# MLP2's second product shared out by products instead of by token tiles

## The chip, the cores and the metric

One NeuronCore of one Trainium2 chip runs the whole program in one launch. The metric is the device time of that launch in microseconds: the median of the timed runs is 855.25 us before the change (three runs, 855.01 to 855.51). The profile is of one further execution of the same kernel, which took 852.9 us and whose instructions span 851.2 us.

## The reference

Windowed attention (4 batches, 8 heads, 576 positions, head size 64; four heads with a window of 32, four with a dilated one) gives x, 2304 tokens by 512. Two MLPs follow, one on the other's result, each with an inner width of 2048:

```
x = attention(q, k, v)                                   # 2304 x 512
h = x @ moe_w_in;   g = where(h > 0, h, exp(min(h, 0)) - 1);   x = g @ moe_w_out
h = x @ moe2_w_in;  g = h * clip(h + 3, 0, 6) / 6;             out = g @ moe2_w_out
```

Inputs and result are float32, and the products hold float32 precision: each operand is split into a high part (rounded to the matmul's format) and a low part (the rest), and three matmuls (high-high, high-low, low-high) stand for one.

## The kernel before

**Stages.** Attention and MLP1 run together over five blocks of tokens (up to about 470 us of the profile). Then MLP2 runs over NC = 3 blocks c of 768 tokens. Both of its products use Strassen's scheme in Winograd's form: a product of 2x2 blocks is made from seven products k = 0 to 6 of sums of blocks instead of eight. The inner width 2048 is walked in KP = 8 steps j of 256.

**The first product** (`gemm2nd`, L932) makes, for a block c and a step j, seven products of 128x384 (six matmuls each, L956) in a chain through three PSUM banks q, p, r; ScalarE copies q aside (L983), VectorE adds (L991), ScalarE and VectorE apply the activation (L1001, L1007). The result is the tile g of step j. Its weights stream from DRAM through a ring `w` of six buffers of 512 KB (`ws_i`, L911); the right operands x lie in SBUF, loaded per block (L879).

**The second product** (`tile2`, L1040) goes by token tiles: i = 0, 1, 2, each of two rows of 128 tokens. For one tile and one step, VectorE forms five sums of g's blocks (L1055, L1059, L1061), ScalarE casts the high parts (`ga`, `gz`, L270), VectorE or GpSimd forms the low parts (L273), and TensorE runs 7 products x 3 passes = 21 matmuls of 256 columns (L1094). The seven results of a tile, 1 KB per partition each, accumulate over the eight steps in four PSUM banks. Four of the seven right operands (`w`, L922) stay in SBUF for all blocks; the other three stream through the ring `w` too (`ws_x`), 12 loads of 512 KB for a pass over all steps, and there are two passes per block: one for tiles 0 and 1 together, one for tile 2.

**Order.** In each block the first product comes first. Tiles 0 and 1 then run alone and fill all eight banks. Tile 2 runs beside the next block's first product (4 banks and the q, p, r of that product); after the last block it runs alone. During the first product of block 1 the right operands of block 2 are also made (`rights`, L784): loads `xq`, sums, casts, stores `rhs`. At the end of a tile `y2_out` (L1156) combines the seven sums into four quarters of output (two ScalarE copies, L1188, eight VectorE adds, L1193) and stores each as 128 KB.

**Who decides the order.** `Plan.run` (L122) simulates the five engines and the DMA queue with fixed costs when the program is built. Each job has a key (its due time, here from `times2`, L828); an engine takes the ready job of the smallest key unless another can start clearly earlier. What it chooses is the order in which each engine's instructions are written; on the chip every engine then works through its list in order and waits for its semaphores. All DMAs are issued by SyncE (SP) on one queue. A DMA's end is assumed as issue + 1.4 us + its own share of the queue + 1.6 us (L190, L191). Rings of buffers (`y` with five, shared by MLP1, the temporaries t and the outputs; `ghl`, `gz`, `ga` with three each) hold a writer back until a buffer is free.

**The 16 loads of resident weights** (`load_w1`, L915) take the place of MLP1's second weights, and are free to go as each of those is used for the last time.

Of the kernel before, what the change touches and what calls it, by code (L numbers as in the profile page):

```python
# [20 lines left out]
P = 128  # L21
# [17 lines left out]
CFG = dict(  # L39
    LAGT=0.23, LAGE=0.07, LAND=1.6,  # L40
# [9 lines left out]
    BUFS=dict(y=5, ghl=3, q=1, k=1, v=1, pt=1, g=8, w=6, gz=3, ga=3),  # L50
    WARM=46.0,
    FROM=1.6,
    END=2, ENDW=8,
# [3 lines left out]
    LAG2=1,  # L57
# [142 lines left out]
def tile_window_attention_two_mlps(  # L200
# [50 lines left out]
    w2d = (  # L251
        dram.tile([P, KP * 7, 2, EH], F32, name="w2di"), dram.tile([P, KP * 4, 2, EH], F32, name="w2do"),
        dram.tile([P, KP * 3, 2, EH], F32, name="w2dx"),
    )
# [11 lines left out]
    RINGS["all"] = Ring(list(BANKS.values()))  # L266
    ENG = {"D": nc.vector, "A": nc.scalar, "P": nc.gpsimd}
# [93 lines left out]
    def stage(key, x, dst, users, need, n=EH, pool=stg, ring="stg"):  # L361

        r = {}

        def hi(e):
            r["w"] = take(pool, ring, [P, 2, n], F32R, f"stg{next(turns)}")
# [5 lines left out]
        su = []  # L372
# [35 lines left out]
    def weights2(j, key, step):  # L408
# [4 lines left out]
        def pair(z, k0, dst, steps):  # L413
# [14 lines left out]
            1, key + step * 0.25, lambda k: w2d[1][:, 4 * j + k] if k < 4 else w2d[2][:, 3 * j + k - 4], (  # L428
# [246 lines left out]
    def tile1(b, i):  # L675
# [34 lines left out]
        def hi(e):  # L710
            r["g"] = take(gp, "ghl", [P, 2, T1], F32R, f"ghl{b}_{i}")
            copy(e, r["g"][:, 0, :], r["e"])
# [15 lines left out]
        hu, eu, gu = Users(), [], []  # L728
# [58 lines left out]
    def rights_of(c, p, k0, start, pool, ring, spool, sring):  # L787

        r, us = {}, [[], []]
        after = [*start] + [x2_done[n, k] for n in range(NB1) for k in (p, p + 2) if A1[n] < (c + 1) * 2 * N1 and A1[n + 1] > c * 2 * N1]  # L790

        def load(e):
            for n in range(2):
                r[n] = take(pool(), ring, [P, 2, N1], F32, f"xq{c}_{p}_{n}")
# [4 lines left out]
        ld = job(k0 - 6.0, load, {"S": 0.84}, after, 2.0, [(RINGS[ring], u) for u in us])  # L799
        for u in us:  # L800
            u.append(ld)
        t = {f"b{n + 1}{h + 1}": lambda n=n, h=h: r[n][:, h] for n in range(2) for h in range(2)}

        def put(k, x, key, users, need):
# [8 lines left out]
            k0, 0.3, t, {v: us[int(v[1]) - 1] for v in t}, dict.fromkeys(t, [ld]), (  # L813
# [11 lines left out]
    GEMM, TILE = 42 * C["R"](N1), 21 * C["R"](EH)  # L825
    MM = 6 * C["R"](N1)

    def times2():  # L828

        t = TB[NB1]  # L830
        for c in range(NC):
            rest = [(c - 1, 2, j) for j in range(KP)] if c else []
            if rest:
                second2[rest[0]] = t, t + 12 * C["R"](EH)
                t += TILE
            for j in range(KP):
                first2[c, j] = t
                if j + 1 < len(rest):
                    second2[rest[j + 1]] = t - 0.1, t + 4.5 * MM
                period2[c, j] = GEMM + (TILE if j + 1 < len(rest) else 0.0)  # L840
                t += period2[c, j]
            t -= 2 * MM
            L = CFG["LAG2"]
            for j in range(KP + L):
                for i, n in ((0, j), (1, j - L)):
                    if 0 <= n < KP:
                        second2[c, i, n] = t, t + 12 * C["R"](EH)
                        t += TILE
# [40 lines left out]
    def load_stream():  # L889
# [6 lines left out]
        for c, i, j in second2:  # L896
            for k in range(3):
                m = "x", c, 0 if i < 2 else 2, (3 * j + k) // 2
                uses[m] = min(uses.get(m, 1e9), second2[c, i, j][0])
        prev = start3  # L900
        for m, key in sorted(uses.items(), key=lambda x: x[1]):
            n = m[-1]
            src, done = (
                (w2d[0], [w2_done[0, x // 7, x % 7] for x in (2 * n, 2 * n + 1)]) if m[0] == "i" else
                (w2d[2], [w2_done[1, x // 3, 4 + x % 3] for x in (2 * n, 2 * n + 1)])
            )
# [8 lines left out]
    def load_w1(i):  # L915
        j, k = divmod(i, 2)
        key = min(second2[0, 0, j][0], second2[0, 1, j][0]) - 30.0
# [7 lines left out]
        w2j[i, 1] = job(key + 0.1, load, {"S": 0.42}, [last[1], *(w2_done[1, j, 2 * k + c] for c in range(2))], 1.3, [(RINGS["w1"], u)])  # L925
# [114 lines left out]
    def tile2(c, i, j):  # L1040

        b = NG * c + i
        k1, k2 = second2[c, i, j]
        lead = k1 - CFG["LEAD2"]
        r = {}

        parts = lambda: g_t[c, j].rearrange("p k t i n -> p (k t) i n")[:, :, i]

        def sums(n):
            def fn(e):  # L1050
                if n == 0:
                    r["f"] = take(gp, "ghl", [P, 5, P], F32, f"gf{b}_{j}")
                z, f = parts(), r["f"]
                if n == 0:
                    ENG[e].tensor_tensor(  # L1055
                        out=f[:, 0:2], in0=z[:, 0:2], in1=z[:, 3:4].to_broadcast([P, 2, P]), op=ALU.add
                    )
                elif n == 1:
                    ENG[e].tensor_tensor(out=f[:, 2], in0=z[:, 0], in1=z[:, 2], op=ALU.add)  # L1059
                else:  # L1060
                    ENG[e].tensor_tensor(out=f[:, 3:5], in0=z[:, 1:3], in1=z[:, 0:4:3], op=ALU.subtract)  # L1061
            return fn

        def a_hi(e):
            r["a"] = take(p2["z"], "ga", [P, 2, 2, P], F32R, f"ga{b}_{j}")
            copy(e, r["a"][:, 0], parts()[:, 0:4:3])

        def a_lo(e):
            sub(e, r["a"][:, 1], parts()[:, 0:4:3], r["a"][:, 0].bitcast(F32))

        def z_hi(e):
            r["z"] = take(p2["z"], "gz", [P, 2, 5, P], F32R, f"gz{b}_{j}")
            copy(e, r["z"][:, 0], r["f"])

        def z_lo(e):
            sub(e, r["z"][:, 1], r["f"], r["z"][:, 0].bitcast(F32))

        def g2(banks):
            def fn(e):
                ms = ys.setdefault(("m", b), {})  # L1080
                for n in banks:
                    if j == 0:
                        y = ps.tile([P, 2, EH], F32, tag=m_users[b][n].tag, name=f"m{b}_{n}")
                        for z, (k, _, _) in enumerate(PRODS[n]):
                            ms[k] = y[:, z]
                    for z, (k, ka, kb) in enumerate(PRODS[n]):
                        if kb < 4:
                            w = w_t[1, 2 * j + kb // 2, 1][:, kb % 2]
                        else:
                            m = 3 * j + kb - 4  # L1090
                            w = stream["x", c, 0 if i < 2 else 2, m // 2][:, m % 2]
                        for s, (a, v) in enumerate(PASSES):
                            g = r["a"][:, a, ka] if ka < 2 else r["z"][:, a, ka - 2]
                            nc.tensor.matmul(  # L1094
                                ms[k], g, w[:, v, :], start=(j == 0 and z == 0 and s == 0),
                                stop=(j == KP - 1 and z == len(PRODS[n]) - 1 and s == 2),
                            )
            return fn

        fu, au, zu = [], [], []  # L1100
        gd = g_done[c, j] + ([x for k in rights_done if k[0] == 2 for x in rights_done[k]] if (c, i, j) == (1, 0, 0) else [])
        o = lambda n: {"D": C["D"](n), "P": C["P"](n)}
        before = LAST.get("sums")
        gate = gates.get((c, i, j))
        s = [job(lead, sums(0), {"D": C["D"](N2)}, [*gd, before and (before, -9.0), gate and (gate, -9.0)], 0, [(RINGS["ghl"], fu)])]
        LAST["sums"] = s[0]
        s += [job(lead + 0.01 * n, sums(n), o(P) if n == 1 else {"D": C["D"](N2)}, [s[0]]) for n in (1, 2)]
        j5 = job(lead + 0.1, a_hi, {"A": C["A"](N2)}, gd, 0, [(RINGS["ga"], au)])
        j6 = job(lead + 0.15, z_hi, {"A": C["A"](5 * P)}, s, 0, [(RINGS["gz"], zu)])
        j7 = job(lead + 0.2, a_lo, o(N2), [j5])  # L1110
        j8 = job(lead + 0.3, z_lo, {"D": C["D"](5 * P)}, [j6])
        g_users[c, j] += [*s, j5, j7]
        fu += [*s, j6, j8]
        prev = LAST.get(b) if j or i == 2 else prod[c, KP - 1, 3]
        if j == 0:
            m_users[b] = [Users() for _ in PRODS]
        xs = [("x", c, 0 if i < 2 else 2, n) for n in sorted({(3 * j + k) // 2 for k in range(3)})]
        need = [j7, j8, w2j[2 * j, 1], w2j[2 * j + 1, 1], *(stream_j[m] for m in xs)]
# [270 lines left out]
```

## Time and profile before

| | |
|---|---|
| median of the runs | 855.25 us (855.01 to 855.51) |
| profiled execution, its span | 852.9 us, 851.2 us |
| TensorE busy | 828.0 us (97%), 5749 matmuls |
| VectorE, ScalarE, GpSimd busy | 606.9 us (71%), 453.1 us (53%), 51.2 us (6%) |
| DMA | 227.85 MB, mean 268 GB/s |
| granted TensorE clock, mean | 0.995 |
| streamed loads in MLP2 | 84 `ws_i` and 72 `ws_x`, 512 KB each |

Busy shares are means over stages with different limits. In MLP2 the stages are, in us of the span: first product of block 0 from about 470 to 537, tiles 0 and 1 alone to 578, block 1's first product with tile 2 to 668, alone to 710, block 2's first product with tile 2 to 788, and all that is left of the second product to 847.

### The profile page before, as it was taken

The numbers are of one execution on the slowest core, as the hardware profiler recorded it, in microseconds if no ns is written. First come the engines' busy times: TensorE is split into PE (matmuls) and PEld (weight loads), VectorE is DVE, ScalarE is ACT, GpSimd is POOL, SyncE is SP. The second block draws the span as 40 slices with busy tenths as digits, with TensorE's granted clock in tenths as the row PEclk, the third lists the DMA queues.
The fourth block names the chain that finished last, engine by engine and source line by source line (L and its number), as shares of the span: only waits on it lengthen the run. The fifth ranks groups of instructions, "written<-read, shape, count | busy, mean of one in ns | idle before, by whom it ended". The sixth has DMA issues, their size and how long they took to land.

```text
span 851.2 us, 15721 instructions
## 1 busy us (share of the span) xinstructions
PE 828.0 (97%) x5749; PEld 749.2 (88%) x5749; DVE 606.9 (71%) x1337; ACT 453.1 (53%) x1048; POOL 51.2 (6%) x85
## 2 busy tenths in 40 slices
PE   7999999999999999999999799999999999999997
PEld 6888888888888888888899799999899999999997
DVE  5998878777777777666456285677767878656796
ACT  3999766666566767452344254444445444444442
POOL 2000010000100000000000000000101000000010
PEclk9999999999999999999999999999999999999999
DMA  9994457787777787644699987969989958888456
GB/s 355 407 368 168 144 197 271 241 261 234 237 268 264 257 270 236 228 120 144 230 356 377 352 273 243 401 197 321 384 285 373 397 193 293 271 260 285 143 170 232
DMA packets 85452, 227.85 MB, mean 268 GB/s; under 512 B 9088, under 2 KB 21376, under 8 KB 85376
## 3 DMA queue, kind: packets, MB, share of 16 engines
q1 hardware_dynamic: 85376, 226.86, 76.6%
q8 instruction: 45, 0.74, 0.3%
q14 instruction: 31, 0.25, 0.1%
HBM read 171.51 MB, written 55.31 MB: 266 GB/s over the span
## 4 chain that ended last, share of the span: by engine, by line
PE 89%; DMA 7%; DVE 1%; ACT 1%; issue 0%; SPq 0%; DVEq 0%; ACTq 0%
PE h L667 23%; PE yp L723 23%; PE m L1094 19%; PE cq L956 11%; PE cr L956 6%; DMA ws_i<-w2di 3%; PE cp L956 3%; PE po L583 2%; PE ps L509 2%; DMA raw<-in_w_in_dram 1%; DMA x2d<-y 1%; DMA ws_x<-w2dx 1%; DMA k<-in_k_dram 1%; PE pp L559 1%; DVE o L1193 0%
## 5 line engine op out<-in xcount | busy, mean ns | idle before, releaser
L723 PE MATMUL yp<-ghl,w 128*128 128x512 f32 (+1 forms) x960 | 213.3, 371 | 0.0
L667 PE MATMUL h<-xh,w 128*128 128x512 f32 (+1 forms) x640 | 195.4, 371 | 1.8 <-DVE e L701 1.6
L723 PEld LDWEIGHTS yp<-ghl,w 128*128 128x128 f32 x960 | 166.3, 189 | 30.0
L667 PEld LDWEIGHTS h<-xh,w 128*128 128x128 f32 x640 | 117.2, 189 | 22.2 <-DVE e L701 1.8
L956 PE MATMUL cq<-x,ws_i 128*128 128x384 f32 x576 | 115.8, 344 | 7.1 <-ACT t L983 5.0
L667 PE MATMUL h<-xl,w 128*128 128x512 f32 (+1 forms) x320 | 117.8, 368 | 0.0
L956 PEld LDWEIGHTS cq<-x,ws_i 128*128 128x128 f32 x576 | 102.0, 190 | 10.1 <-ACT t L983 6.8
L687 ACT ACTIVATE e<-h 128x512 f32<-128x512 f32 (+1 forms) x80 | 44.4, 555 | 121.3 <-PE h L667 117.6
L701 DVE SCALAR_TENSOR_TENSOR e<-e,h 128x512 f32<-128x512 f32 (+1 forms) x80 | 50.5, 632 | 69.4 <-ACT e L690 69.1
L1094 PE MATMUL m<-w,gz 128*128 128x256 f32 x648 | 95.1, 283 | 0.0
L270 ACT CAST gz<-gf 128x640 fp32r<-128x640 f32 x72 | 52.1, 727 | 80.3 <-PE m L1094 62.4
L1094 PEld LDWEIGHTS m<-w,gz 128*128 128x128 f32 x648 | 86.0, 192 | 0.0
L273 DVE TENSOR_TENSOR gz<-gf,gz 128x640 fp32r<-128x640 f32 x72 | 59.6, 830 | 29.6 <-ACT gz L270 29.2
L667 PEld LDWEIGHTS h<-xl,w 128*128 128x128 f32 x320 | 60.4, 189 | 9.8 <-DVE xl L590 0.3
L983 ACT COPY t<-cq 128x384 f32<-128x384 f32 x72 | 34.4, 478 | 60.9 <-PE cq L956 52.6
L1001 ACT ACTIVATE g<-t 128x384 f32<-128x384 f32 x72 | 37.8, 525 | 51.2 <-DVE t L991 51.2
L1094 PE MATMUL m<-ws_x,gz 128*128 128x256 f32 x432 | 63.5, 283 | 0.0
L956 PE MATMUL cr<-x,ws_i 128*128 128x384 f32 x288 | 57.9, 345 | 0.6 <-DMA ws_i<-w2di 0.6
L1007 DVE SCALAR_TENSOR_TENSOR g<-g,t 128x384 f32<-128x384 f32 x72 | 40.4, 560 | 24.3 <-ACT g L1001 23.3
L1094 PEld LDWEIGHTS m<-ws_x,gz 128*128 128x128 f32 x432 | 57.0, 192 | 0.0
L273 DVE TENSOR_TENSOR ghl<-e,ghl 128x512 fp32r<-128x512 f32 (+1 forms) x80 | 50.9, 637 | 3.7 <-ACT ghl L270 1.3
L956 PEld LDWEIGHTS cr<-x,ws_i 128*128 128x128 f32 x288 | 52.6, 194 | 0.9 <-DMA ws_i<-w2di 0.9
(89 smaller groups left out, 1170.0 us busy)
## 6 DMA issues: line engine op xcount, KB each, us to landing
ws_i<-w2di SPq DMA_DIRECT2D x84, 512.0 KB, 4.9
ws_x<-w2dx SPq DMA_DIRECT2D x72, 512.0 KB, 5.2
raw<-in_w_in_dram SPq DMA_DIRECT2D x32, 512.0 KB, 6.1
raw<-in_w_out_dram SPq DMA_DIRECT2D x32, 512.0 KB, 5.9
x<-rhs SPq DMA_DIRECT2D x42, 384.0 KB, 8.2
w2di<-stg SPq DMA_DIRECT2D x56, 256.0 KB, 4.5
rhs<-stg SPq DMA_DIRECT2D x28, 384.0 KB, 6.1
q<-in_q_dram SPq DMA_DIRECT2D x18, 512.0 KB, 5.7
```

Source lines behind the costliest of these rows:

```text
L270: (nc.scalar.copy if e == "A" else nc.vector.tensor_copy)(out=out, in_=in_)
L273: ENG[e].tensor_tensor(out=out, in0=in0, in1=in1, op=ALU.subtract)
L509: nc.tensor.matmul(pe[c * KW:(c + 1) * KW, n, :], t["q"][:, c, n, :], kk[:, c], start=not pe_masks, stop=not pe_masks or n == NB - 1)
L667: nc.tensor.matmul(h, w[:, a, c * P:(c + 1) * P], x[b][:, c, :], start=(c == 0 and s == 0), stop=(c == KD - 1 and s == 2),)
L687: nc.scalar.activation(out=r["e"], in_=r["h"], func=AF.Relu, scale=-1.0)
L701: nc.vector.scalar_tensor_tensor(out=r["e"], in0=r["e"], scalar=-1.0, in1=r["h"], op0=ALU.add, op1=ALU.max)
L723: nc.tensor.matmul(ys[b, n], w[:, a, n * P:(n + 1) * P], g[:, c, :], start=(i == 0 and s == 0), stop=(i == KF - 1 and s == 2),)
L956: nc.tensor.matmul(r[b], w[:, a, p * P:(p + 1) * P], x2[c, k, p][:, z, :], start=start and p == 0 and n == 0, stop=p == 1 and n == 2, skip ...
L983: nc.scalar.copy(out=r[n], in_=r[b])
L1001: nc.scalar.activation(out=g_t[c, j][:, k, t].rearrange("q i n -> q (i n)"), in_=r[src], func=AF.Relu, bias=3.0)
L1007: nc.vector.scalar_tensor_tensor(out=z, in0=z, scalar=6.0, in1=r[src], op0=ALU.min, op1=ALU.mult)
L1094: nc.tensor.matmul(ms[k], g, w[:, v, :], start=(j == 0 and z == 0 and s == 0), stop=(j == KP - 1 and z == len(PRODS[n]) - 1 and s == 2),)
```

## The change

The second product is shared out by products. In each block, the five products 3, 2, 4, 0, 1 run alone for all three tiles together (pass `b`), and products 5 and 6 run for all three tiles beside the next block's first product (pass `e`), after the last block alone. One job is now one product of one step for three tiles: PART = 9 matmuls of 256 columns. The number of matmuls is the same.

- PSUM: products 3, 2, 4, 0, 1 of tiles 0 and 1 take a bank each; tile 2's halves pair up in banks "32", "40", "1x" (eight banks). Pass `e` takes three: "5", "6" and "56" for tile 2. A half of tile 2 is read once the later product of its bank is done.
- Operands: sums are 384 wide, one per product (`plus`, three in pass `b`); `less` overwrites two blocks of g in place before pass `e`. The high and low parts of each product go through one ring `gc` of seven buffers (the three of `ghl` and four new ones).
- Streamed weights: pass `b` needs one of the three (4 loads of 512 KB per block), pass `e` two (8 loads): 12 per block in place of 24.
- Outputs: a ring `o` of nine buffers of 128 KB in place of `y`. All three tiles' outputs are combined at the end of pass `b` (6 copies, 18 adds of one quarter each); the quarters (1,1) and (0,0) then wait in their buffers for products 5 and 6.
- Loads: a resident weight with i >= 6 is put behind the first product of step (i - 6) // 2 of block 0, less 9 us of the plan. The two loads of `xq` become two jobs, and block 2's right operands are staged through `gc`.

```diff
-    BUFS=dict(y=5, ghl=3, q=1, k=1, v=1, pt=1, g=8, w=6, gz=3, ga=3),
+    BUFS=dict(y=5, ghl=3, q=1, k=1, v=1, pt=1, g=8, w=6, gc=4, o=9),
+    PASS = dict(b=((3, 1, 4), (2, 0, 3), (4, 4, 1), (0, 2, 2), (1, 3, 0)), e=((5, 5, 6), (6, 6, 5)))
+    HALF = {3: ("32", 0), 2: ("32", 1), 4: ("40", 0), 0: ("40", 1), 1: ("1x", 0), 5: ("56", 0), 6: ("56", 1)}
...
+            if c:
+                second2[c - 1, "e", 0] = t, t + PART
+                t += 2 * PART
             for j in range(KP):
                 first2[c, j] = t
+                period2[c, j] = GEMM
+                if c and j + 1 < KP:
+                    second2[c - 1, "e", j + 1] = t - 0.1, t + 4.5 * MM
+                    period2[c, j] += 2 * PART
                 t += period2[c, j]
             t -= 2 * MM
+            for j in range(KP):
+                second2[c, "b", j] = [t + n * PART for n in range(5)]
+                t += 5 * PART
             t += 2 * MM
...
+        gate = [(prod[0, (i - CFG["W1G"]) // 2, 0], -9.0)] if i >= CFG["W1G"] else []
+        w2j[i, 1] = job(key + 0.1, load, {"S": 0.42}, [last[1], *gate, *(w2_done[1, j, 2 * k + c] for c in range(2))], 1.3, [(RINGS["w1"], u)])
...
+            def less(e):
+                x = g_t[c, j].rearrange("p k t i n -> p (k t) (i n)")
+                ENG[e].tensor_tensor(out=x[:, 1:3], in0=x[:, 1:3], in1=x[:, 0:4:3], op=ALU.subtract)
...
+            x = job(lead + 0.1, hi, {"A": C["A"](N1)}, [*need, *gate, LAST.get("gc") and (LAST["gc"], -9.0)], 0, [(RINGS["gc"], zu)])
+            y = job(lead + 0.2, lo, {"D": C["D"](N1), "P": C["P"](N1)}, [x])
...
+                for i in range(NG):
...
+                    for s, (a, v) in enumerate(PASSES):
+                        nc.tensor.matmul(
+                            ms[c, k, i], r["z"][:, a, i * P:(i + 1) * P], w[:, v, :], start=(c, nm) in opened, stop=end and s == 2,
+                        )
...
+            f10 = step(1 + i, i, (1, 0), 3, scaled(i, (1, 0), 3), a)
+            f11 = step(2 + i, i, (1, 1), 2, scaled(i, (1, 1), 2), a)
+            x = step(3 + i, i, (0, 0), 4, add(i, (0, 0), (1, 0), 4, -1.0), d, [f10])
+            y = step(4 + i, i, (0, 1), 4, add(i, (0, 1), (1, 1), 4), d, [f11])
+            store(5, i, (0, 1))
+            step(6 + i, i, (0, 0), 0, add(i, (0, 0), (0, 0), 0), d)
+            step(7 + i, i, (1, 1), 0, add(i, (1, 1), (1, 1), 0), d, [y])
+            step(8 + i, i, (1, 0), 1, add(i, (1, 0), (1, 0), 1), d, [x])
+            store(9, i, (1, 0))
+            step(10 + i, i, (1, 1), 1, add(i, (1, 1), (1, 1), 1, -1.0), d)
```

## Rows read from the trace of the kernel before

**Rows 1.** Windows by stage: length, busy us (instructions) per engine, PEclk, DMA share, GB/s

```profile
484.00:537.00 53.00, 51.70 (x283) 51.37 (x284) 35.09 (x73) 26.77 (x57) 0.93 (x2) 0.97 0.79 267
537.00:578.00 41.00, 41.00 (x341) 41.00 (x340) 30.90 (x76) 17.93 (x36) 0.23 (x1) 1.00 0.77 269
578.00:668.00 90.00, 86.64 (x542) 84.88 (x541) 66.76 (x145) 42.34 (x90) 8.95 (x10) 0.98 0.97 355
668.00:710.00 42.00, 41.24 (x341) 41.07 (x340) 34.46 (x86) 17.99 (x36) 2.91 (x4) 1.00 0.76 258
710.00:788.00 78.00, 77.31 (x489) 76.70 (x488) 50.29 (x105) 34.13 (x71) 3.12 (x5) 1.00 0.85 284
788.00:842.00 54.00, 54.00 (x452) 53.91 (x450) 44.96 (x110) 23.81 (x47) 2.96 (x4) 1.00 0.65 205
```

**Rows 2.** PE's timeline in MLP2: start, us, line, operation, [idle before, releaser]

```profile
480.15 1.32 PE L956 MATMUL cr<-x,ws_i 128*128 128x384 f32 x6 [0.58 <-DMA ws_i<-w2di]
484.68 2.25 PE L956 MATMUL cq<-x,ws_i 128*128 128x384 f32 x6 [3.20 <-ACT t L983]
486.72 1.88 PE L956 MATMUL cr<-x,ws_i 128*128 128x384 f32 x6
488.44 3.34 PE L956 MATMUL cq<-x,ws_i 128*128 128x384 f32 x18
...
535.82 1.33 PE L956 MATMUL cq<-x,ws_i 128*128 128x384 f32 x6 [0.62 <-ACT t L983]
...
583.83 1.29 PE L956 MATMUL cq<-x,ws_i 128*128 128x384 f32 x6 [0.49 <-DMA ws_i<-w2di]
...
616.39 1.32 PE L956 MATMUL cp<-x,ws_i 128*128 128x384 f32 x6 [2.07 <-DMA ws_i<-w2di]
...
682.62 0.59 PE L1094 MATMUL m<-ws_x,ga 128*128 128x256 f32 x3 [0.76 <-ACT gz L270]
...
842.62 0.59 PE L1094 MATMUL m<-ws_x,ga 128*128 128x256 f32 x3 [0.51 <-DMA ws_x<-w2dx]
```

**Rows 3.** Windows, columns as in Rows 1: the stretch after the 2.07 us gap

```profile
618.00:628.00 10.00, 10.00 (x57) 10.00 (x56) 5.04 (x10) 4.25 (x9) 1.13 (x1) 0.84 0.71 233
```

**Rows 4.** The chain that ended last, in order of time: start, us, what

```profile
473.77 10.30 DMA x2d<-y
...
538.20 39.24 PE m L1094 x327
```

**Rows 5.** SP's timeline around MLP2's start: start, us, DMAs issued

```profile
468.73 0.45 SPq L922 DMA_DIRECT2D w<-w2do  x1
...
473.77 0.32 SPq L280 DMA_DIRECT2D x2d<-y  x1
475.05 0.32 SPq L922 DMA_DIRECT2D w<-w2do  x1
```

**Rows 6.** DMA issues from 578 to 668 us: count, KB each, median us to landing

```profile
ws_x<-w2dx SPq DMA_DIRECT2D x14, 512.0 KB, 6.4
...
out_dram<-o SPq DMA_DIRECT2D x8, 128.0 KB, 5.3
```

**Rows 7.** Groups by line and form: count, busy us, mean ns, idle before

```profile
L273 DVE TENSOR_TENSOR stg<-xq,stg 128x384 fp32r<-128x384 f32 x28 | 15.3, 556 | 2.2 <-ACT stg L270 1.9
```

**Rows 8.** DVE's timeline while tiles 0 and 1 run alone

```profile
561.66 0.83 DVE L273 TENSOR_TENSOR gz<-gf,gz 128x640 fp32r<-128x640 f32 x1
562.40 0.75 DVE L1055 TENSOR_TENSOR gf<-g 128x256 f32<-128x256 f32 x2
563.08 0.28 DVE L1059 TENSOR_TENSOR gf<-g 128x128 f32<-128x128 f32 x1
```

**Rows 9.** Timeline around a GpSimd instruction in block 1's first product

```profile
611.29 1.13 POOL L273 TENSOR_TENSOR ga<-g,ga 128x256 fp32r<-128x256 f32 x1 [13.65 <-ACT ga L270]
...
611.74 0.83 DVE L1059 TENSOR_TENSOR gf<-g 128x128 f32<-128x128 f32 x1
```

**Rows 10.** Timeline of the end: the last adds and the last stores

```profile
845.10 2.93 DVE L1193 SCALAR_TENSOR_TENSOR o<-m,o 128x256 f32<-128x256 f32 x8 [4.56 <-PE m L1094]
845.89 2.65 SPq L280 DMA_DIRECT2D out_dram<-o  x4
```

More of the change, by code (lines that the diff above doesn't have):

```diff
@@ L39 @@
 CFG = dict(
+    W1G=6,
     LAGT=0.23, LAGE=0.07, LAND=1.6,
@@ L250, in tile_window_attention_two_mlps @@
     rhs = dram.tile([P, NC, 7, 2, 2, N1], F32, name="rhs")
[L251 to L254, printed above, removed]
+    w2d = [
+        dram.tile([P, KP * n, 2, EH], F32, name=f"w2d{x}") for x, n in (("i", 7), ("o", 4), ("b", 1), ("e", 2))
+    ]
     plan = Plan()
@@ L365, in hi @@
         def hi(e):
-            r["w"] = take(pool, ring, [P, 2, n], F32R, f"stg{next(turns)}")
+            nm = f"stg{next(turns)}"
+            r["w"] = grab(su, [P, 2, n], F32R, nm) if su.tag else take(pool, ring, [P, 2, n], F32R, nm)
             copy(e, r["w"][:, 0], x())
@@ L787, in rights_of, with load @@
     def rights_of(c, p, k0, start, pool, ring, spool, sring):
-        r, us = {}, [[], []]
+        r, us = {}, [Users(), Users()]
         after = [*start] + [x2_done[n, k] for n in range(NB1) for k in (p, p + 2) if A1[n] < (c + 1) * 2 * N1 and A1[n + 1] > c * 2 * N1]
-        def load(e):
-            for n in range(2):
-                r[n] = take(pool(), ring, [P, 2, N1], F32, f"xq{c}_{p}_{n}")
+        ld = []
+        for n in range(2):
+            def load(e, n=n):
+                nm = f"xq{c}_{p}_{n}"
+                r[n] = grab(us[n], [P, 2, N1], F32, nm) if us[n].tag else take(pool(), ring, [P, 2, N1], F32, nm)
                 nc.sync.dma_start(
@@ L797, in load @@
                 )
-        ld = job(k0 - 6.0, load, {"S": 0.84}, after, 2.0, [(RINGS[ring], u) for u in us])
-        for u in us:
-            u.append(ld)
+            ld.append(job(k0 - 6.0 + 0.01 * n, load, {"S": 0.42}, after, 1.0, [(RINGS[ring], us[n])]))
+            us[n].append(ld[n])
         t = {f"b{n + 1}{h + 1}": lambda n=n, h=h: r[n][:, h] for n in range(2) for h in range(2)}
@@ L1038, in gemm2nd @@
         act(0, 1, 1, [c12], tu[1], K(6) + 0.6)
[L1040 to L1049, printed above, removed]
-            def fn(e):
[L1051 to L1118, printed above, removed]
-        use = [au, zu, w_users[1, 2 * j, 1], w_users[1, 2 * j + 1, 1], *(stream_u[m] for m in xs)]
-        au += [j5, j7]
-        zu += [j6, j8]
-        gu = []
-        if (c, i) == (NC - 1, 2) and j >= KP - CFG["END"]:
-            ends.append((g2, need))
-            end_users.extend(use)
-            if j == KP - 1:
-                last = []
-                for n in range(len(PRODS)):
-                    size = 3 * len(PRODS[n])
-                    for g, nd in ends:
-                        prev = job(
-                            k1 + 0.01 * n, g((n,)), {"T": size * C["R"](EH)}, [*need, *nd, prev], 0, ()
-                        )
-                    last.append(prev)
-                for u in end_users:
-                    u += last
-                y2_out(b, k1 + 2.5, last)
-            return
-        for n, (banks, size) in enumerate((((0, 1), 12), ((2, 3), 9))):
-            prev = job(
-                (k1, k2)[n], g2(banks), {"T": size * C["R"](EH)}, [*need, prev], 0,
-                [(RINGS["all"], m_users[b][k]) for k in banks] if j == 0 else (),
-            )
-            gu.append(prev)
-        LAST[b] = prev
-        for u in use:
-            u += gu
-        if j == KP - 1:
-            y2_out(b, k2 + 1.1, [gu[0], gu[0], gu[1], gu[1]])
```

261 lines of the change are left out of this document (159 added, 102 removed).

## The prediction

> **What bounds the kernel now.** I read the page's busy shares first (TensorE 97%, so only its idle time and its slower stretches can be won), then the chain of waits, then the windows by stage, then TensorE's own timeline for each gap, and last the queue's timeline behind the gaps that a DMA ended. In MLP2 the reader is to see stages in which TensorE is full: 41.00 of 41 us with tiles 0 and 1 alone, 54.00 of 54 in the last stretch [rows 1]. Its rate is that of the matmuls: 39.24 us for 327 is 0.120 us for one of 256 columns [rows 4], and 18 of 384 columns in the 3.18 us from 488.44 to the next group are 0.177 us each [rows 2]. MLP2 has 3 x 8 x 42 = 1008 of the wide and 3 x 8 x 63 = 1512 of the narrow ones: 178 + 181 = 359 us, and the change keeps every one. So the question is only which gaps go and which come.
>
> There are four kinds of gap [rows 2]. (1) At MLP2's start TensorE stands 0.58 us for streamed weights and 3.20 us for a ScalarE copy. That copy waited for a buffer of ring `y`, held by a store x2d<-y that took 10.30 us from issue to landing [rows 4] because loads stood ahead of it in the one queue. (2) In block 1's first product it stands 0.49 and 2.07 us for streamed weights, where the DMA share is 0.97 at 355 GB/s, against 0.85 and 284 GB/s in block 2's, which has no such gap [rows 1]. (3) Single ones at 682.62 (0.76, operands) and 842.62 (0.51, `ws_x`). (4) A gap of about 0.6 us late in each first product, waiting for the copy before product 5 (535.82 is one of three).
> A long gap costs more than itself. After the 3.20 us, twelve wide matmuls took 3.76 us (484.68 to 488.44 [rows 2]) where 2.12 is normal: 1.6 us lost. After the 2.07 us the next 10 us were granted 0.84 of the clock [rows 3], a mix of its 1.2 and 2.4 GHz levels, which is again 10 x 0.16 = 1.6 us.
>
> **The change, part by part.**
> Start of MLP2. Of the 16 resident loads, four are issued between 468.73 and 475.05, three ahead of the store issued at 473.77 [rows 5]. The new gate lets loads 6 and 7 go when the first product of step 0, less 9 us, is due (470.5 + 1.1 - 9, about 463), 8 and 9 one step of 7.4 us later (about 470), 10 and 11 at 477, the rest later. So two, not three, stand ahead of that store. One load of 512 KB (0.524 MB) at 355 GB/s is 1.5 us, so the copy comes 1.5 us earlier. Bounds: 0 if the plan puts three there again; 0.58 + 3.20 + 1.6 = 5.4 us if the store lands in time. I take 1.5, the nearest row. Moved loads cost nothing: they fall into block 0's first product, at a DMA share of 0.79 [rows 1].
>
> Block 1's first product. Pass `e` takes 8 loads where tile 2 took 12, and pass `b` before it 4 where tiles 0 and 1 took 12. In the window 14 `ws_x` are issued [rows 6]; nine are left (eight of `e`, one of the next `b`), 5 x 0.524 = 2.6 MB less of the 32 MB. More important, a `b` load serves two steps (10 x 1.08 = 10.8 us), so near the end of pass `b` the ring of six holds one or two of them, and four or five loads of the next stage come ahead of it (another 2 MB). About 27.4 of 32 MB in the same stretch is 305 GB/s, near block 2's 284, where no DMA gap is. So I let both gaps and the slow stretch go: 0.49 + 2.07 + 1.6 = 4.2 us. Bounds 0 and 4.2.
>
> Single gaps. At 842.62 the load in question belonged to a stream of 12 loads; pass `e` has 8: 0.5 us goes. At 682.62 the operands came late out of a ring of three whole tiles; with seven single buffers I take half, 0.4 us. Sum 0.9, bounds 0 and 1.3. The three gaps of 0.6 us stay: the chain before product 5 is untouched. Bounds for these, from gone to doubled: -1.8 to +1.8.
>
> Operands on VectorE. An instruction's duration overlaps the next: 640 wide is 0.83 us but the next starts after 0.74, and 256 wide follows at 0.34 (0.75 us for two, the next 0.68 after their start) [rows 8]. A 384-wide one is 0.556 [rows 7], less 0.08 is 0.475; `less`, 768 wide, by the slope between 256 and 640 about 0.89 (estimate). Pass `b` needs eight of 384 per step: 3.8 us in 5.4 us of TensorE, 70%; before it was 30.90 of 41 us, 75% [rows 1]. Pass `e` alone: 0.89 + 2 x 0.475 = 1.84 in 2.16 us. Block 1's first product: 8 x (7 x 0.475 + 1.84) + 24 x 0.475 for block 2's operands + 24 adds x 0.36 = 41 + 11 + 9 = 61 us in at least 77. Nothing becomes bound; 0 us. The tightest place is the last pass `e`: eight steps (14.7 us) and 18 adds (6.5 us) in the 17.3 us of `e` and the 7.5 us that seven buffers allow ahead: 21.2 of 24.8. Bounds 0 and +2.
> GpSimd is no help in that sum: while its 1.13 us instruction ran from 611.29, a 128-wide VectorE instruction took 0.83 us instead of 0.28 [rows 9]. The Trainium skill says so too (SBUF — State Buffer, Who interferes with whom): a VectorE instruction with two SBUF inputs and a GpSimd one that reads SBUF exclude each other. By that rule four low parts given to GpSimd, as in the last stretch now [rows 1], would cost VectorE some 4 x (1.2 - 0.475) = 3 us more, 24 of 24.8. I leave the sum at 0, because the plan also counts the two as exclusive.
>
> Outputs at the end of pass `b`. Call this end T. Twelve quarters of output are wanted at once and ring `o` has nine. Six copies take six; the adds for two of (0,0) and the first (0,1) take the rest, at about T - 1.2 (product 4 ends at T - 2 x 1.08, then three adds at 0.36). The next (0,1) must wait for the store of the first. The plan takes that store to land 0.42 + 1.4 + 0.4 + 1.6 = 3.8 us after issue; such stores took 5.3 us in this stretch [rows 6]. VectorE stands in order behind it for up to 1.5 us, with the adds that free the banks "0", "1", "40", "1x", and with them the next first product's q, p, r. TensorE's cover is the prepared products of pass `e`, 1.08 us each. I take half of the 1.5 us, 0.7 at each of the two ends that a first product follows: +1.4. Bounds 0 and +8.6 (below). Under zero is excluded: the 0.49 us gap there is already counted.
>
> The end. Now eight adds end at 848.03 and the last of four stores is issued by 848.54 [rows 10]. Afterwards tiles 0 and 1 of product 6 and both halves of tile 2 are left after the last matmul, four adds and four stores, one pair of them later than now: +0.3, bounds 0 and +1.
>
> **Sum.** -1.5 - 4.2 - 0.9 + 0 + 1.4 + 0.3 = -4.9 us. The profiled execution took 852.9 us, its span 851.2 with 1.7 around it; 852.9 - 4.9 = 848.0. The median of the runs stands 2.35 us above the profiled one, so 850.4 us.
>
> **The rivals.**
> A. *Banks come too late (slower).* If TensorE has no products of pass `e` prepared beyond step 0, it runs dry at T + 2.16 while the second (0,1) waits until T - 1.2 + 5.3 = T + 4.1, and bank "1" is free two or three adds later, T + 4.9 or more: 2.7 us of standing and 1.6 us of slow clock, 4.3 at each of two ends, 8.6. With the gains of 6.6 and the 0.3 kept: 855.25 - 6.6 + 0.3 + 8.6 = 857.6. It decides from fewer than three prepared products on (2.7 / 1.08). For it speaks the nine against twelve, and that (1,1) is chained behind (0,1); against it that `gc` has seven buffers and VectorE 30% to spare in pass `b`.
> B. *The loads are fewer, but the gaps stay.* The gaps of kind (2) lie in the first 40 us, where xq, rhs and the outputs, which the change leaves or adds to (six stores at once), share the queue with `ws_i`. Then 4.2 us stay: 854.6. For it speaks that only 14 of the loads there were `ws_x`; against it block 2's stage at 284 GB/s.
> C. *More is won.* The gate clears the start wholly and the plan covers every bank: -5.4 - 4.2 - 1.3 + 0.3 = -10.6, 844.7. For it speaks that half of the resident loads move; against it that seven streamed loads stand ahead of the store in any case.
>
> **Chances.** Forecast 0.55, A 0.17, B 0.13, C 0.15. About 0.2%, 1.7 us, is what a measurement here can tell from no change. Faster: most of the forecast (0.50) and C, 0.66 with a little of B. Same (853.5 to 857.0): most of B, a third of A, the forecast's upper edge, 0.18. Slower: the rest of A and mishaps not named, 0.16. The range runs from C's 845 to just over A's 857.6: 845 to 858.
>
> **What would show it.** Right: no idle above 0.3 us ended by ws_i in block 1's first product, its DMA share under 0.95, no window there under 0.95 of the clock; 36 streamed loads of the second product in place of 72; x2d<-y landing 1 to 2 us earlier. For A: VectorE's adds waiting for out_dram<-o after pass `b` and TensorE's cq or cp waiting for VectorE's adds within 6 us of it. For B: ws_i ending gaps as now. The prediction is wrong in substance if TensorE's idle time in the stages of pass `b` or the last pass `e` grows by more than 2 us, which I hold at none.

## The result and the profile after

The changed kernel takes 841.38 us (median of four runs, 838.94 to 842.06) against 855.29 of the kernel before: ratio 0.9832, 95% interval 0.9812 to 0.9853. Two later comparisons of the same two kernels gave 0.9861 (0.9838 to 0.9883) and 0.9838 (0.9815 to 0.9861). The forecast was 850.4 us, in a range from 845 to 858: the sign was right, the gain is about three times the one forecast, and the time lies below the range. The profiled execution took 838.94 us, its span 837.0, so the two profiled spans lie 851.2 - 837.0 = 14.2 us apart.

The page of the changed kernel: its span, the busy shares, and a group of the first and of the second product, with the idle time before them. This group of the first product waits 3.7 us in all, the products of pass `e` never (`ws_b` and `ws_e` are the streamed weights of the two passes, `gc` their operands).

```profile
span 837.0 us, 15622 instructions
PE 822.1 (98%) x5749; PEld 746.0 (89%) x5749; DVE 598.2 (71%) x1238; ACT 465.6 (56%) x1080; POOL 54.6 (7%) x80
...
L967 PE MATMUL cq<-x,ws_i 128*128 128x384 f32 x576 | 113.7, 339 | 3.7 <-DMA x<-rhs 2.6
L1129 PE MATMUL m<-ws_e,gc 128*128 128x256 f32 x432 | 56.2, 283 | 0.0
```

The windows by stage, columns as in [rows 1] and answering to them: block 0's first product, pass `b`, block 1's first product with pass `e`, pass `b`, block 2's, pass `b`, the last pass `e`.

```profile
484.00:535.00 51.00, 50.81 (x298) 50.40 (x297) 32.40 (x58) 25.95 (x56) 5.32 (x5) 1.00 0.94 353
535.00:578.00 43.00, 43.00 (x357) 43.00 (x356) 36.42 (x70) 21.59 (x46) 0.00 (x0) 1.00 0.48 172
578.00:655.00 77.00, 76.26 (x482) 76.02 (x481) 56.76 (x116) 39.84 (x85) 7.23 (x7) 1.00 0.96 349
655.00:698.00 43.00, 43.00 (x358) 43.00 (x357) 37.37 (x72) 22.48 (x47) 0.00 (x0) 1.00 0.48 178
698.00:775.00 77.00, 76.79 (x486) 76.52 (x485) 44.94 (x90) 34.43 (x71) 8.07 (x8) 1.00 0.78 258
775.00:818.00 43.00, 43.00 (x361) 43.00 (x360) 37.91 (x72) 22.49 (x47) 2.03 (x2) 1.00 0.23 67
818.00:838.00 20.00, 14.60 (x122) 14.39 (x120) 8.42 (x22) 3.62 (x8) 3.06 (x3) 0.93 0.36 121
```

All gaps of TensorE from MLP2's start on, out of its timeline; they answer to [rows 2]. Four are left. (The first is put down to `x<-rhs` by the trace; the runs with early loads, below, show that it is a streamed load `ws_i`.)

```profile
468.16 1.30 PE L967 MATMUL cq<-x,ws_i 128*128 128x384 f32 x6 [2.59 <-DMA x<-rhs]
484.40 1.32 PE L967 MATMUL cq<-x,ws_i 128*128 128x384 f32 x6 [0.19 <-ACT t L994]
595.47 1.29 PE L967 MATMUL cq<-x,ws_i 128*128 128x384 f32 x6 [0.74 <-DMA ws_i<-w2di]
753.92 1.29 PE L967 MATMUL cq<-x,ws_i 128*128 128x384 f32 x6 [0.21 <-DVE gc L274]
```

A gap's size leaves out the slower matmuls around it. So I count lost time: from the start of a group of matmuls to the start of the next, less 0.1765 us for each of 384 columns and 0.12 us for each of 256. Summed by stretch over both timelines, one execution of each kernel:

| stretch | lost before | lost after | change | forecast |
|---|---|---|---|---|
| end of MLP1 (one gap at 453.09) | | | -2.2 | none |
| MLP2's start, to 500 us | 7.4 | 3.7 | -3.7 | -1.5 |
| block 1's first product | 5.6 | 0.9 | -4.7 | -4.2 |
| three gaps before product 5 | 2.3 | 0 | -2.3 | 0 |
| single gaps and the rest of the blocks | 2.1 | 0.3 | -1.8 | -0.9 |
| after pass `b` | 0 | 0 | 0 | +1.4 |
| behind the last matmul | 4.0 | 4.4 | +0.4 | +0.3 |
| sum | | | -14.3 | -4.9 |

The first row is the advance with which TensorE reaches MLP2's first product, after counting the twelve `yp` matmuls (the second product of MLP1) that the changed kernel still has to do then. Only 1.64 us of its 2.2 is the gap itself. The gap shows in the windows from 437 to 453 us, of the kernel before and then of the changed one, where TensorE is full:

```profile
437.00:453.00 16.00, 14.45 (x121) 14.25 (x119) 13.83 (x33) 8.72 (x22) 0.00 (x0) 1.00 0.99 364
```

```profile
437.00:453.00 16.00, 16.00 (x136) 16.00 (x135) 12.64 (x31) 8.37 (x22) 0.00 (x0) 1.00 1.01 369
```

### The profile page after: what moved, and what is told of

Its sections match the earlier page's. It is cut to its first block, busy times and chain, and to the rows that moved or that the text cites. A ratio compares the mean times of both kernels' runs of the same rounds, so it can differ in the third digit from the quotient of the medians.

```text
span 837.0 us, 15622 instructions
## 1 busy us (share of the span) xinstructions
PE 822.1 (98%) x5749; PEld 746.0 (89%) x5749; DVE 598.2 (71%) x1238; ACT 465.6 (56%) x1080; POOL 54.6 (7%) x80
## 4 chain that ended last, share of the span: by engine, by line
PE 95%; DMA 3%; ACT 1%; DVE 1%; SPq 0%; issue 0%; DVEq 0%
PE yp L730 24%; PE h L674 24%; PE m L1129 20%; PE cq L967 12%; PE cr L967 6%; PE cp L967 3%; PE po L590 2%; PE ps L516 2%; DMA raw<-in_w_in_dram 1%; PE m_1x L1129 1%; PE pp L566 1%; DMA k<-in_k_dram 1%; DMA ws_i<-w2di 1%; DMA x<-rhs 0%; PE fill L1269 0%; SPq L472 0%
## 5 line engine op out<-in xcount | busy, mean ns | idle before, releaser
L967 PE MATMUL cq<-x,ws_i 128*128 128x384 f32 x576 | 113.7, 339 | 3.7 <-DMA x<-rhs 2.6
L1129 PE MATMUL m<-w,gc 128*128 128x256 f32 x792 | 101.1, 283 | 0.0
L1129 PEld LDWEIGHTS m<-w,gc 128*128 128x128 f32 x792 | 98.1, 192 | 0.0
L271 ACT CAST gc<-g 128x384 fp32r<-128x384 f32 x96 | 49.1, 514 | 42.6 <-PE m L1129 27.8
L274 DVE TENSOR_TENSOR gc<-g,gc 128x384 fp32r<-128x384 f32 x85 | 47.6, 562 | 20.6 <-ACT gc L271 19.1
L271 ACT CAST gc<-gf 128x384 fp32r<-128x384 f32 x72 | 36.9, 514 | 40.9 <-PE m L1129 36.2
L1129 PE MATMUL m<-ws_e,gc 128*128 128x256 f32 x432 | 56.2, 283 | 0.0
L967 PE MATMUL cr<-x,ws_i 128*128 128x384 f32 x288 | 55.3, 338 | 0.0
L1129 PEld LDWEIGHTS m<-ws_e,gc 128*128 128x128 f32 x432 | 54.7, 191 | 0.1
```

Source lines behind the costliest of these rows:

```text
L271: (nc.scalar.copy if e == "A" else nc.vector.tensor_copy)(out=out, in_=in_)
L274: ENG[e].tensor_tensor(out=out, in0=in0, in1=in1, op=ALU.subtract)
L967: nc.tensor.matmul(r[b], w[:, a, p * P:(p + 1) * P], x2[c, k, p][:, z, :], start=start and p == 0 and n == 0, stop=p == 1 and n == 2, skip ...
L1129: nc.tensor.matmul(ms[c, k, i], r["z"][:, a, i * P:(i + 1) * P], w[:, v, :], start=(c, nm) in opened, stop=end and s == 2,)
```

## The experiments

Each run stands beside runs of the kernel before on the same chip. The changed kernel's own three ratios differ by 0.003, so two ratios that lie closer than this don't tell two kernels apart; there the traces must. The lost time of a stretch differs between executions of one kernel too: in the changed kernel's three profiles it is 3.7, 3.6 and 5.0 us at MLP2's start, and 0.9, 1.6 and 5.5 us in block 1's first product.

**The gate on the resident loads, taken away.**

```diff
-    W1G=6,
+    W1G=16,
```

> The changed kernel without the gate on the resident loads (W1G = 16, so every load goes as soon as its buffer is free, as before). Theory G, the gate empties the queue at MLP2's start: the 1.64 us gap late in MLP1 and the 3.2 us wait of a ScalarE copy for the store x2d<-y come back with their slow clock, 846 to 848 us. Rival, the finer jobs let TensorE work around late loads there: under 843 us, with no gap over 1 us beside the one for the first weights.

Measured: 842.79 us, ratio 0.9879 (0.9859 to 0.9899). At MLP2's start streamed weights are late again:

```profile
477.24 1.29 PE L967 MATMUL cp<-x,ws_i 128*128 128x384 f32 x6 [0.54 <-DMA ws_i<-w2di]
479.79 1.32 PE L967 MATMUL cr<-x,ws_i 128*128 128x384 f32 x6 [1.26 <-DMA ws_i<-w2di]
481.98 1.32 PE L967 MATMUL cq<-x,ws_i 128*128 128x384 f32 x6 [0.86 <-ACT t L994]
```

The time lost to 500 us is 6.2 us, not 3.7, and nothing before it has changed: no gap at 453 us. So the gate gives 2.5 us in these two executions, at the start alone, and what it clears first are the streamed loads `ws_i`; the copy that I had reasoned about is the third of these waits (ScalarE stood 7.40 us before it for the store x2d<-y). Of theory G the wait for the copy came back, smaller, and the gap in MLP1 and the 846 us did not; the rival's time held, but not its "no gap over 1 us".

**The gate alone, in the kernel before.**

```diff
-        w2j[i, 1] = job(..., [last[1], *(w2_done[...] ...)], ...)
+        w2j[i, 1] = job(..., [last[1], *([(prod[0, (i - 6) // 2, 0], -9.0)] if i >= 6 else []), *(w2_done[...] ...)], ...)
...
```

The jobs of these loads are also created later, behind those of block 0's first product that the gate names, as in the changed kernel.

> The kernel before with the gate on the resident loads alone, nothing else changed. Theory G: most of the two gaps goes, 849 to 851 us, and x2d<-y lands within 7 us. Rival, without the finer jobs the gate is worth little: 853.5 us or more.

Measured: 851.56 us, ratio 0.9975 (0.9957 to 0.9993), 2.2 us less than before on this chip. Its time lost at the start is 5.1 us against 7.4 (forecast by theory G: 849 to 851 us; x2d<-y lands within 4.8 us, as it said); all the other gaps stay:

```profile
453.55 0.39 PE L667 MATMUL h<-xh,w 128*128 128x256 f32 x1 [1.64 <-DVE e L701]
...
533.85 1.33 PE L956 MATMUL cq<-x,ws_i 128*128 128x384 f32 x6 [0.62 <-ACT t L983]
...
616.10 1.32 PE L956 MATMUL cp<-x,ws_i 128*128 128x384 f32 x6 [2.48 <-DMA ws_i<-w2di]
```

The two runs agree: the gate is worth 2.3 to 2.5 us, in either kernel, a sixth of the gain. The medians say the same of the kernel before (2.2 us); for the changed kernel they leave 1.5 to 4 us.

**Twice the streamed loads in passes `b` and `e`.**

```diff
-            m = (h, c, j // 2) if h == "b" else (h, c, j)
-            uses[m] = min(uses.get(m, 1e9), second2[c, h, j][0])
+            for z in range(1 if h == "b" else 2):
+                uses[h, c, z, j] = second2[c, h, j][z]
...
```

> The changed kernel with as many streamed loads of the second product as before, 24 per block instead of 12: each load of 512 KB now serves one product of one step, so half of its bytes are not used. Theory L, fewer loads cleared block 1's first product: gaps ended by ws_i come back there, 3 to 4 us, 844 to 846 us. Rival, the finer jobs cleared it: within 1 us of the changed kernel.

Measured: 847.18 us, ratio 0.9925 (0.9906 to 0.9944): 5 to 8 us more than the changed kernel, by the comparison taken. In block 1's stage the DMA engines are full and TensorE waits again, for the pass's own loads:

```profile
578.00:655.00 77.00, 74.96 (x466) 73.57 (x465) 55.19 (x111) 39.42 (x83) 8.90 (x8) 1.00 1.01 388
```

```profile
596.08 1.33 PE L1130 MATMUL m<-ws_e,gc 128*128 128x256 f32 x9 [0.62 <-DMA ws_e<-w2de]
618.58 1.33 PE L1130 MATMUL m<-ws_e,gc 128*128 128x256 f32 x9 [0.79 <-DMA ws_e<-w2de]
...
835.74 1.30 PE L1130 MATMUL m<-ws_e,gc 128*128 128x256 f32 x9 [0.55 <-DMA ws_e<-w2de]
```

By stretch, its lost time over the changed kernel's is 2.6 us in block 1, 1.3 in block 2, 1.5 at the start (where no load was added) and 3.1 in the last pass `e`: 8.5 us, where the spans differ by 8.3. What this run shows is that doubled loads cost time, more than either expectation had, and 3.1 us of it in the last pass, which with two loads for each 2.16 us of matmuls is a case of its own that the kernel before never had. That fewer loads carry block 1's term is likely, not shown: the doubled loads bring back about half of it, by waits for `ws_e` and not for `ws_i` as theory L had it, and the changed kernel itself lost more there (5.5 us) and as much at the start (5.0) in another execution.

**Hard borders between the passes.** Pass `b` waits for the whole first product, and the next first product and pass `e` wait for pass `b`.

```diff
-                need.append(LAST["mm"] if n else prod[c, KP - 1, 3])
+                need.append(LAST["mm"] if n else prod[c, KP - 1, 6])
+            if h == "e" and not j and not n:
+                need += [done2[c, x] for x in (3, 2, 4, 0, 1)]
...
+        for c in range(1, NC):
+            for k in (0, 1, 3):
+                prod[c, 0, k].need.append((done2[c - 1, 1], 0.0))
```

> The changed kernel with hard borders: pass b begins after the last product of the first product, and the next block's first product and pass e begin after the last job of pass b. Theory B, jobs of one product and three tiles let the plan mix the stages and so fill the waits at the borders: the three gaps of 0.6 us come back (1.8 us) and TensorE waits for banks after pass b, 2 to 4 us with slow clock at two ends, 845 to 851 us in all. Rival, the banks are free in time without it: 843 to 844 us, the three gaps alone.

Measured: 842.11 us, ratio 0.9866 (0.9849 to 0.9883). The three gaps before product 5 are back, and after pass `b` there is still no wait for a bank:

```profile
530.37 1.33 PE L967 MATMUL cq<-x,ws_i 128*128 128x384 f32 x6 [0.62 <-ACT t L994]
...
651.60 1.33 PE L967 MATMUL cq<-x,ws_i 128*128 128x384 f32 x6 [0.62 <-ACT t L994]
...
772.56 1.33 PE L967 MATMUL cq<-x,ws_i 128*128 128x384 f32 x6 [0.62 <-ACT t L994]
```

In the changed kernel the place of the first of these looks as follows: a product of pass `b`, 1.08 us of matmuls that want nothing from the chain, stands between two first products.

```profile
528.06 1.22 PE L967 MATMUL cq<-x,ws_i 128*128 128x384 f32 x6
529.12 1.24 PE L1129 MATMUL m<-ws_b,gc 128*128 128x256 f32 x9
530.20 1.22 PE L967 MATMUL cq<-x,ws_i 128*128 128x384 f32 x6
```

So the small jobs fill the three gaps (2.3 us in the traces), and of the expectations the rival's came: the three gaps alone (843 to 844 us expected). Against the changed kernel's three ratios the difference in time is within what they vary by; the trace shows it, not the median.

**The xq loads as one job again.** The change also split the load of two xq tiles, one buffer each, into two jobs.

```diff
-        for n in range(2):
-            def load(e, n=n):
+        def load(e):
+            for n in range(2):
...
-            ld.append(job(k0 - 6.0 + 0.01 * n, load, {"S": 0.42}, after, 1.0, ...))
+        ld = [job(k0 - 6.0, load, {"S": 0.84}, after, 2.0, ...)] * 2
...
```

> The changed kernel with the two loads of xq as one job again. The 1.64 us gap late in MLP1 is not the gate's: it stayed with the gate alone and is gone in the changed kernel without the gate. Theory X, the split of the loads removes it, since the first sums need not wait for the second load: the gap is back at about 453 us, 1.5 to 2 us slower than the changed kernel. Rival, it goes with the named buffers of ring ghl: no gap over 0.5 us there, within 0.5 us of the changed kernel.

Measured: 844.62 us, ratio 0.9889 (0.9868 to 0.9909), beside 0.9861 of the changed kernel on that chip: 1.7 us more, as theory X had it, though two ratios this close don't show it. The gap of MLP1 is back to the hundredth:

```profile
452.69 0.39 PE L674 MATMUL h<-xh,w 128*128 128x256 f32 x1 [1.64 <-DVE e L708]
```

VectorE's timeline says how. With one job, nine instructions on xq in a row (448.00 to 452.23) stand ahead of one `e` that TensorE needs; the first fence is this run, the second the changed kernel, where an `e` stands right behind the first sum of xq (L406).

```profile
451.76 0.55 DVE L274 TENSOR_TENSOR stg<-xq,stg 128x384 fp32r<-128x384 f32 x1
452.23 0.41 DVE L708 SCALAR_TENSOR_TENSOR e<-e,h 128x256 f32<-128x256 f32 x1
```

```profile
448.04 0.56 DVE L406 TENSOR_TENSOR xq<-xq 128x384 f32<-128x384 f32 x1
448.51 0.41 DVE L708 SCALAR_TENSOR_TENSOR e<-e,h 128x256 f32<-128x256 f32 x1
```

**Output buffers: seven, eight and ten in place of nine.** The price of rival A, by its own resource.

```diff
-    BUFS=dict(..., gc=4, o=9),
+    BUFS=dict(..., gc=4, o=7),
```

> The changed kernel with seven output buffers in place of nine. Theory A, as the prediction priced it: the adds that free the banks wait for stores, TensorE stands 2 to 4 us after pass b at two ends, 4 to 9 us slower than the changed kernel. Rival C, TensorE has seven prepared products and a plan that puts them there: under 1 us slower, and no gap of TensorE within 10 us of the end of pass b.

> The changed kernel with a ring of eight output buffers, not nine (with seven it was 859.98, ratio 1.0072, two long stalls after pass b). Theory: the ring decides between seven and nine, and with eight the last two quarters of a pass wait for a store that takes about 5 us: a wait of 1 to 3 us at each of the two ends of pass b, 845 to 850 in all. Rival: eight already cover it, 842.

> The changed kernel with a ring of ten output buffers. Theory: with nine no matmul waits for a bank after pass b, so a tenth gains nothing: the changed kernel's 842 within 1 us. Rival: nine only just cover it, and runs in which a store is late lose time; then ten is 1 to 2 us faster in the median.

Measured: seven 859.98 us (ratio 1.0072, 1.0053 to 1.0091), eight 842.92 (0.9863, 0.9840 to 0.9885; the changed kernel beside it 0.9838), ten 841.54 (0.9841, 0.9818 to 0.9864). With seven, VectorE stands 2.52 us for a store, and TensorE 3.07 us for the add behind it; the same again after the next pass `b`:

```profile
594.84 1.34 DVE L1191 SCALAR_TENSOR_TENSOR o<-m,o 128x256 f32<-128x256 f32 x3 [2.52 <-DMA out_dram<-o]
```

```profile
595.32 2.29 PE L967 MATMUL cp<-x,ws_i 128*128 128x384 f32 x6 [3.07 <-DVE o L1191]
```

```profile
595.00:605.00 10.00, 9.68 (x47) 9.68 (x48) 6.35 (x14) 2.89 (x6) 0.00 (x0) 0.83 0.71 214
```

With eight, there are four gaps of 0.57 us, all ended by a copy t; this is the first:

```profile
580.79 1.33 PE L967 MATMUL cq<-x,ws_i 128*128 128x384 f32 x6 [0.57 <-ACT t L994]
```

These sum to 2.3 us, and the median is 2.4 us over the changed kernel's, which is within the intervals: the 845 to 850 expected did not come. The copies themselves waited for nothing but TensorE's own `cq` (VectorE stood at most 0.46 us for a store), so these are not waits for a bank: the plan, made for another ring, put no other product there. With nine there is none. So rival A's mechanism exists, and at seven, gaps of this kind among them, 8.4 and 7.1 us are lost at the two ends, twice the 4.3 each that I gave it. The ring of nine lies behind the bend, and the tenth buffer gains nothing that can be measured.

**The changed kernel twice more**, beside the runs above.

> The changed kernel once more, beside the next three on one chip: ratio to before 0.981 to 0.985 by all theories.

> The changed kernel itself, beside the other three on this chip: 0.983 to 0.986 of the kernel before; what differs from run to run are waits for loads in block 1's first product.

Measured: 842.91 us (839.63 to 845.28) and 840.56 (839.54 to 842.89). The execution of 845.28 us was profiled: its start lost 5.0 us, not 3.7, and block 1's first product 5.5 us, not 0.9, as much as in the kernel before: it has a wait of 1.92 us for ws_e, with 0.83 of the clock from 608 to 618 us, and one of 1.20 us for a copy at 639. The second fence is its whole stage.

```profile
607.64 1.33 PE L1129 MATMUL m<-ws_e,gc 128*128 128x256 f32 x9 [1.92 <-DMA ws_e<-w2de]
```

```profile
578.00:655.00 77.00, 73.68 (x453) 73.02 (x452) 54.72 (x113) 37.85 (x81) 6.24 (x6) 0.98 0.92 322
```

The first of the two expectations, at most 0.985, was missed (0.9861). Block 1's stage is therefore not cleared for good: at a DMA share of 0.92, lower than the 0.96 of the execution above, one late load still cost 2 us and more. What makes a load late in one and not in another isn't settled.

**The first streamed loads of MLP2 early**, in buffers of the w1 ring that are free by then: the first one, and in a second kernel the first two (the condition is then m in (("i", 0, 0), ("i", 0, 1))).

```diff
+            if m == ("i", 0, 0):
+                def load0(e, ...):
+                    w = stream[m] = take(w1p, "w1", [P, 2, 2, EH], F32R, ...)
+                    nc.sync.dma_start(out=w.bitcast(F32), in_=src[:, 2 * n:2 * n + 2])
+                stream_j[m] = job(key - 60.0, load0, ..., [tiles[NB1 - 1, 0][1], *done], 1.3, [(RINGS["w1"], u)])
+                continue
...
```

The resident loads wait for the early ones; the first product keeps its earliest start (`start3`).

> The changed kernel with the first 512 KB of streamed weights (products 0 and 1 of step 0, block 0) loaded early into the first buffer that MLP1's second weights leave; the last resident load takes that buffer afterwards. Theory F, the 2.6 us gap at MLP2's start is the landing of this load, issued only when MLP1's last first product is done: the gap shrinks to under 1 us, 1.5 to 2.5 us faster than the changed kernel. Rival, TensorE then waits for the second load instead: within 0.7 us.

> The changed kernel with the first two streamed loads of MLP2's first product (1 MB) put early into buffers of the w1 ring that are free by then, not the first alone. With one load early the gap at MLP2's start moved to the second load: 2.26 us at 468.77. Theory: the two loads feed 24 matmuls (4.2 us), in which the third load arrives, so the gap goes: about 2 us under the kernel with one early load, ratio about 0.980. Rival: the queue as a whole is late there, the gap moves on to the third load and the time stays at 0.982.

Measured: one load 839.09 us (ratio 0.9823, 0.9806 to 0.9840; the changed kernel beside it 0.9861), two loads 838.56 (0.9811, 0.9791 to 0.9831; beside it 0.9838). The first fence is the kernel with one load, the second that with two. With one, the gap moves to the next load; with two it goes, although the same load `x<-rhs` is issued as late as before, so it was `ws_i` that TensorE waited for. A later first product waits for a copy instead, and that copy for the store x2d<-y, the wait that the prediction began with:

```profile
468.77 1.30 PE L975 MATMUL cq<-x,ws_i 128*128 128x384 f32 x6 [2.26 <-DMA x<-rhs]
```

```profile
483.07 0.48 ACT L1002 COPY t<-cq 128x384 f32<-128x384 f32 x1 [4.01 <-DMA x2d<-y]
483.61 1.32 PE L975 MATMUL cq<-x,ws_i 128*128 128x384 f32 x6 [1.90 <-ACT t L1002]
```

Both are the fastest kernels of the case by their medians, by 2 to 4 us: with one load the rival had the gap right and neither side the time; with two the theory had the gap right, and the ratio lies between the two sides (0.980 and 0.982). The time lost to 540 us is 3.0 us with two loads against 3.6 in the profiled execution of the changed kernel beside it, and both have a span of 837.6 us: the profiles don't show the 2 us. All four runs with two loads (837.84 to 839.36) lie below all four of the changed kernel (839.54 to 842.89), but the two intervals overlap. That it is faster is likely, not shown, and its reason is open.

## Why the prediction was wrong

The bound was read rightly: TensorE's work is unchanged, and the whole gain is idle time and slow stretches. The rate of the matmuls, the tail (+0.4 for +0.3) and VectorE's term of 0 held: no matmul of the last pass `e` waits (818 us on: one gapless run), and block 1's VectorE work is 56.8 us in 77, where I had 61. The forecast failed in these steps:

- **"The three gaps of 0.6 us stay: the chain before product 5 is untouched."** The chain is untouched, but the gap was never the chain's alone: it was the lack of other work to put into it. Before, the second product begins only after the whole first one (538.20 [rows 4]); now single products of pass `b`, 1.08 us each, stand in it. I priced the division into products by its loads and operands and left out that it makes smaller jobs for the plan to place. 2.3 us, shown by the hard borders. My bound of 1.8 for it summed the gaps' sizes; with the 0.16 us by which groups otherwise overlap (six wide matmuls take 1.22 us, the next group starts after 1.06) they were 2.3.
- **"I take half of the 1.5 us, 0.7 at each of the two ends": +1.4.** It cost nothing. I let pass `b` end at one instant T. The plan mixes: cq and products of pass `e` come in from 571.15, before the last of pass `b`, and the adds run through without a wait for a store. The run with hard borders has no wait either, so nine buffers suffice with the three products of pass `e` (27 matmuls at 576.83) that the plan puts there; the mixing was not needed for this.

```profile
571.15 1.22 PE L967 MATMUL cq<-x,ws_i 128*128 128x384 f32 x6
...
573.27 1.24 PE L1129 MATMUL m<-ws_e,gc 128*128 128x256 f32 x9
...
577.23 0.52 PE L1129 MATMUL m_1x<-w,gc 128*128 128x256 f32 x3
```

- **"Two, not three, stand ahead of that store", so -1.5.** -3.7 came. In the changed kernel four resident loads stand ahead of the store, not two, and it is issued at 478.28, not at 473.77 [rows 5]: the count was wrong and was the wrong thing to count. The store lands no earlier either (at least 5.9 us after its issue, 484.2 or later; before at 484.07), against the sign that I had named. What changed is what is late. Six streamed loads now go ahead of the gated resident ones, so the first product runs on: by 484.4 us TensorE has done twelve groups of six wide matmuls, where it had done eight by 484.68 before [rows 2]. And MLP1's last `yp` matmuls, whose result the stores carry, come at 477.32 and not at 472.68; the later they come, the shorter the copy waits for their buffers (8.30 us before, 4.01 with two loads early, where they come at 474.82, none here), though no run changes this alone. The 0.19 us left there is a copy that waited for VectorE, not for a store. By waits, the ones for `ws_i` and for the copy with the slow stretch lost 5.9 us before and 0.5 after, a gain of 5.4 us, just the upper bound that I gave; against it the wait for the first load grew from 1.5 to 2.8, since twelve `yp` matmuls (1.44 us) that filled it before now come later. The gate is 2.3 to 2.5 of the 3.7 (two runs); the other 1.2 came with the rest of the change and was not taken apart. The first fence is ScalarE's copy before, the second the same after.

```profile
484.15 0.48 ACT L983 COPY t<-cq 128x384 f32<-128x384 f32 x1 [8.30 <-DMA x2d<-y]
```

```profile
483.87 0.48 ACT L994 COPY t<-cq 128x384 f32<-128x384 f32 x1 [0.63 <-DVE g L1018]
```

The queue after the change:

```profile
464.17 0.32 SPq L921 DMA_DIRECT2D ws_i<-w2di  x1
464.53 0.42 SPq L889 DMA_DIRECT2D x<-rhs  x1
465.00 2.35 SPq L921 DMA_DIRECT2D ws_i<-w2di  x5
467.39 1.09 SPq L932 DMA_DIRECT2D w<-w2do  x2
470.54 2.69 SPq L921 DMA_DIRECT2D ws_i<-w2di  x2
473.28 0.90 SPq L932 DMA_DIRECT2D w<-w2do  x2
478.28 1.61 SPq L286 DMA_DIRECT2D x2d<-y  x3
```

- **A term that wasn't in the sum: the end of MLP1.** I looked for gaps from MLP2 on, because the change's name says MLP2; the split of the xq loads reaches into the last 30 us of MLP1, where VectorE was 13.83 of 16 us busy. 2.2 us, of which the run with one job shows the 1.64 of the gap.
- **Single gaps, -1.8 for -0.9.** Both named gaps (682.62 and 842.62 [rows 2]) went whole, with the short delays around them; I had taken half of the first. No run takes apart what removed them.

Block 1's term was right in size in the execution beside the result (-4.7 for -4.2): 36 streamed loads in place of 72, and of the waits for `ws_i` one of 0.74 us is left. There is luck in it: the changed kernel's two other profiles lost 1.6 and 5.5 us there, against 5.6 before, and that the loads are the cause is likely only. What I said would show it came out otherwise, a wait for `ws_i` over 0.3 us, a DMA share of 0.96, not under 0.95, and 349 GB/s, not 305. The bytes were as estimated, 349 x 77 = 26.9 MB where I had 27.4, but they move in a window of 77 us, not 90, since part of the stage's work now lies in pass `b`. A share near 1 proves no bound by itself, as the execution with more waits at a share of 0.92 shows; the waits do.

Rival C was the nearest (844.7): it had the start cleared, the single gaps and no bank wait, and lacked the three gaps and MLP1. I gave it 0.15 on the ground that streamed loads stand ahead of the store in any case; they do, and in the changed kernel's profile nobody waits for the store. Rival A was held off by two buffers: with eight no matmul waits for an add, with seven one waits over 3 us at each end.

## What to carry to other kernels

Before pricing a gap as the delay of its chain, ask what else could run in it: cutting a block of work into pieces of about the gap's length, without dependences on that chain, removes gaps that the change doesn't touch. Read every hunk of a change at the place in the timeline where it runs, not only at the place the change is named for; splitting one two-tile load job moved an instruction in another stage's engine order. And profile more than one execution before a single gap is put to a cause: a stage lost 0.9 us in one and 5.5 in another. A ring's price has a bend: here nine buffers cost nothing that shows, eight 2.3 us of gaps in the trace, seven 17 us in the median, so a margin should be asked for in buffers and tried on both sides.

## What the runs showed that I had not expected

A wait costs TensorE more than its length: with seven outputs the window of 10 us that follows the 3.07 us wait was granted 0.83 of the clock, a mix of its 1.2 and 2.4 GHz levels, as behind the 2.07 us gap of before [rows 3]; the time lost around the first pass `b`'s end was 8.4 us. And one and the same kernel differs by 5.7 us between executions on one chip (839.63 to 845.28); in the longest, which was profiled, the difference to the shortest profiled beside the result lies at MLP2's start (5.0 us lost, not 3.7) and in block 1's first product (5.5, not 0.9).
